# The eighth product of each group of eight on 128 rows in place of 64

## The chip, the cores and the metric

One core of a Trainium2 chip runs the kernel. The metric is the device time of one execution in microseconds (us), and lower is better. Several executions of the kernel before are given by their median; one further execution was recorded by the hardware profiler, and all rows below come from that one.

## What is computed

A recurrence over 768 steps (4 batches, 8 heads, head size 40) gives a matrix x of 3072 tokens by 320 features. Two dense layers follow.

```python
def _moe_ref(x, w_in, w_out):           # layer 1: 320 -> 2048 -> 320
    h = x @ w_in
    g = np.where(h >= 1.0, h, np.where(h <= -1.0, 0.0, (h + 1.0) ** 2 / 4.0))
    return g @ w_out

def _moe2_ref(x, w1, w2, w3, w_out):    # layer 2: 320 -> 3 x 768 -> 320
    h = np.maximum(np.maximum(x @ w1, x @ w2), x @ w3)
    return h @ w_out
```

All data is float32, and the result is float32.

## The kernel before

The recurrence is worked in 24 chunks of 32 steps (`front` and `back`, called from `build` for each chunk). Its products are small: many of them use a part of the TensorE array only, with 32, 40, 64, 96 or 104 rows and 32 or 40 columns (lines 462, 587, 607, 629, 664 and 684). A long run of small VectorE operations for each chunk (lines 487 to 513) belongs to it too.

The dense layers are done in a split form. A float32 operand is written as a high part and a low part in TensorE's rounded float32 type, and a product is the sum of high by high, high by low and low by high. For the 320 input features this makes a group of eight products that add up in one PSUM tile. Features 0 to 127 and 128 to 255 take two full slices of 128 rows each. The last 64 features stand in slice 4 of the weights, with the high part on rows 0 to 63 and the low part on rows 64 to 127; the activations hold the same 64 features twice, on rows 0 to 63 and again on rows 64 to 127 (the last 64 columns are copied behind the others before the transpose, at the end of `back` for layer 1 and by a second small DMA in `moe2`). So one product over 128 rows, the third in the list, gives both high by high and low by high for the last 64 features. The eighth product adds high weights by low activations for them, on rows 0 to 63 only.

Layer 1 (`moe1`) takes 256 tokens at a time, in 12 units. Each unit has 16 groups of eight (line 818, moving operand of 256 columns), in eight pairs; a pair is followed by an activation on ScalarE (line 824), a square (line 825 or GpSimd), a VectorE operation (line 826), the split of the result into gH and gL, and 12 products of line 840 that add into two output tiles. That is 192 groups in all. Layer 2 (`moe2`) takes 512 tokens at a time, in 6 units. Each has 18 groups of eight (line 954, 512 columns, 108 groups in all), three for each of six column blocks; ScalarE and VectorE form the maximum of the three and its high and low part (fH, fL, held in the memory of the layer-1 weights, so that the profile calls them "wi"), and line 980 multiplies them with the output weights, 18 products for each of 4 token blocks.

The order of the work is fixed when the program is built. A planner (`Plan`) gives each task a duration and starts tasks in a list order on every engine; a group of eight is entered with 8 x 109 ns in layer 1 (line 821) and 8 x 216 ns in layer 2 (line 956). The order that comes out is written into each engine's stream, and engines wait for one another by semaphores. In idle stretches of the plan the kernel issues filler products on the identity matrix (line 1009), without waits. Groups of layer 1 stand between the recurrence's products in TensorE's stream; the last unit of layer 1 and then layer 2 follow when the recurrence is done.

Of the kernel before, what the change touches and what calls it, by code (L numbers as in the profile page):

```python
# [210 lines left out]
def act(n):  # L211
    return 94 + n * 0.833
# [6 lines left out]
def dve(n):  # L219
    return 68 + n / 0.96  # L220
# [6 lines left out]
def pool(n):  # L227
    return 98 + n * 2.2


def ev(n):

    return (("ACT", acp(n)), ("DVE", dve(n)))
# [6 lines left out]
class Kernel:  # L240
# [557 lines left out]
    def moe1(self, u):  # L798
        nc, P = self.nc, self.P
        i2 = u % 2  # L800
        xk = [("xH", i2, c) for c in range(2)] + [("xL", i2, c) for c in range(2)]
        wi, wo = self.wi, self.wo
        og = [Group("out") for _ in range(2)]
        self.hm = []
        for mp in range(8):
            g = Group("b6" if u == 11 else "h")
            j = (u * 8 + mp) % 2
            for mm in range(2):
                m = mp * 2 + mm

                def hm(e, m=m, mm=mm, g=g):
                    p = self.bank[g.bank][:, mm * 256:(mm + 1) * 256]
                    ms = slice(m * 128, (m + 1) * 128)
                    xH, xL = self.xH[i2], self.xL[i2]
                    seq = [(wi[:, 0, ms], xH[:, 0]), (wi[:, 1, ms], xH[:, 1]), (wi[:, 4, ms], xH[:, 2]), (wi[:, 2, ms], xH[:, 0]),
                           (wi[:, 3, ms], xH[:, 1]), (wi[:, 0, ms], xL[:, 0]), (wi[:, 1, ms], xL[:, 1]), (wi[0:64, 4, ms], xL[0:64, 2])]
                    for i, (a, b) in enumerate(seq):
                        nc.tensor.matmul(p, a, b, start=(i == 0), stop=(i == 7))  # L818

                f = m // 4  # L820
                self.hm.append(P.add((("PE", 8 * 109.0),), hm, r=xk + [("wi", kt, f) for kt in range(5)], g=[g]))
            q = self.q[j]
            bv = lambda g=g: self.bank[g.bank].rearrange("p (a b) -> p a b", a=2)
            P.add((("ACT", act(512)),), lambda e, q=q, bv=bv: nc.scalar.activation(q, bv(), AF.Relu, bias=self.half, scale=0.5), w=[("q", j)], g=[g])  # L824
            P.add((("ACT", act(512)), ("POOL", pool(512))), lambda e, q=q: nc.scalar.square(q, q) if e == "ACT" else self.tt(e, q, q, q, ALU.mult), w=[("q", j)])  # L825
            P.add((("DVE", dve(512)),), lambda e, q=q, bv=bv: nc.vector.scalar_tensor_tensor(q, bv(), 1.0, q, ALU.max, ALU.min), w=[("q", j)], g=[g])  # L826
            P.add((("ACT", act(512)),), lambda e, q=q, j=j: self.copy(e, self.gH[j], q), r=[("q", j)], w=[("gH", j)])
            P.add((("POOL", pool(512)), ("DVE", dve(512)))[u == 11:], lambda e, q=q, j=j: self.tt(e, self.gL[j], q, self.gH[j].bitcast(F32), ALU.subtract),
                  r=[("q", j), ("gH", j)], w=[("gL", j)])
            for mm in range(2):  # L830
                m = mp * 2 + mm

                def om(e, m=m, mm=mm, j=j):
                    gH, gL = self.gH[j], self.gL[j]
                    for tg in range(2):
                        p = self.bank[og[tg].bank][:, 0:DM]
                        ts = slice(tg * 128, (tg + 1) * 128)
                        seq = [(gH[:, mm, ts], wo[:, m, 0]), (gH[:, mm, ts], wo[:, m, 1]), (gL[:, mm, ts], wo[:, m, 0])]
                        for i, (a, b) in enumerate(seq):
                            nc.tensor.matmul(p, a, b, start=(m == 0 and i == 0), stop=(m == 15 and i == 2))  # L840

                P.add((("PE", 6 * 136.0),), om, r=[("gH", j), ("gL", j), ("wo", m, 0), ("wo", m, 1)], w=["moe1"], g=og)
        for tg in range(2):
            c = u * 2 + tg
            xt = self.x2n[0]
            P.add(ev(320), lambda e, tg=tg, xt=xt: self.copy(e, xt, self.bank[og[tg].bank][:, 0:DM]), w=["x2n"], g=[og[tg]], bonus=1e6)
            self.dma(self.x2d[c], xt, r=["x2n"], w=[("x2d", c)], bonus=1e6)
# [66 lines left out]
    def moe2(self, u):  # L914
# [27 lines left out]
        for m in range(6):  # L942
            ms = slice(m * 128, (m + 1) * 128)
            k2 = (u * 6 + m) % 2
            early = u == 0 and m == 0
            gs = [Group("a" if early else "b6") for _ in range(3)]
            for j in range(3):
                def mm(e, j=j, ms=ms, g=gs[j]):
                    p = self.bank[g.bank]
                    w, yH, yL = tl["w3"], tl["yH"][i2], tl["yL"][i2]  # L950
                    seq = [(w[:, j, 0, ms], yH[:, 0]), (w[:, j, 1, ms], yH[:, 1]), (w[:, j, 4, ms], yH[:, 2]), (w[:, j, 2, ms], yH[:, 0]),
                           (w[:, j, 3, ms], yH[:, 1]), (w[:, j, 0, ms], yL[:, 0]), (w[:, j, 1, ms], yL[:, 1]), (w[0:64, j, 4, ms], yL[0:64, 2])]
                    for i, (a, b) in enumerate(seq):
                        nc.tensor.matmul(p, a, b, start=(i == 0), stop=(i == 7))  # L954

                t = P.add((("PE", 8 * 216.0),), mm, r=yk + [("w3", j, kt, m // 3) for kt in range(5)] + ([] if early else ["moe1"]), g=[gs[j]])
                if self.mm:
                    t.deps.add(self.mm)
                self.mm = t
            P.add((("ACT", act(512)),), lambda e, k2=k2, gs=gs: self.copy(e, tl["s1"][k2], self.bank[gs[0].bank]), w=[("s1", k2)], g=[gs[0]])  # L960
            P.add((("DVE", dve(512)),), lambda e, k2=k2, gs=gs: self.tt(e, tl["s2"][k2], tl["s1"][k2], self.bank[gs[1].bank], ALU.max), r=[("s1", k2)], w=[("q", k2)], g=[gs[1]])
            P.add((("DVE", dve(512)),), lambda e, k2=k2, gs=gs: self.tt(e, tl["s1"][k2], tl["s2"][k2], self.bank[gs[2].bank], ALU.max), r=[("q", k2)], w=[("s1", k2)], g=[gs[2]])
            sm = sl[m]
            t = P.add((("ACT", act(512)),), lambda e, k2=k2, m=sm: self.copy(e, tl["fH"][:, m], tl["s1"][k2]), r=[("s1", k2)], w=[("fH", sm)])
            if u < 2:
                t.deps.update(self.hm)
            P.add((("DVE", dve(512)),), lambda e, k2=k2, m=sm: self.tt(e, tl["fL"][:, m], tl["s1"][k2], tl["fH"][:, m].bitcast(F32), ALU.subtract),
                  r=[("s1", k2), ("fH", sm)], w=[("fL", sm)])
# [240 lines left out]
```

## Time and profile before

| | |
|---|---|
| median of 3 executions | 1240.98 us (1238.32 to 1241.63) |
| the profiled execution | 1236.07 us |
| its span, first to last instruction | 1234.3 us |
| TensorE matmul busy | 1108.8 us, 90% |
| TensorE weight loads busy | 924.8 us, 75% |
| VectorE busy | 817.2 us, 66% |
| ScalarE busy | 719.7 us, 58% |
| GpSimd busy | 385.5 us, 31% |

In the profile PE is the matmul side of TensorE, PEld its weight load side, DVE is VectorE, ACT ScalarE, POOL GpSimd, SPq the queue that issues DMAs. L818 is line 818 of the kernel. "128*128" before a shape gives the rows and columns of the array that an instruction uses. PE's matmuls are pipelined: each row shows a start and a duration, and the durations overlap, so the spacing of starts tells the rate. PEclk is the granted clock of TensorE as a share of its full 2.4 GHz; 0.50 is the level of 1.2 GHz.

### The profile page before, as it was taken

To read this page: it belongs to the slowest core of one execution; us is meant where nothing else is said; L and a number is where in the kernel's file an instruction comes from. 1 tells how busy PE (TensorE), PEld (TensorE's weight loads), DVE (VectorE), ACT (ScalarE), POOL (GpSimd) and SP (SyncE) were. 2 spreads that over 40 slices of the span, in tenths; PEclk is the share of its full clock that TensorE was granted. 3 is DMA by queue.
4 is the path that set the end of the run, shared out by engine and by line. 5 is a ranking of instruction groups with operands and counts; after the bars stand their busy time and mean duration, and the time that the engine had idled before them with its cause. 6 is when DMAs were issued, how large, how long until landed. Compare 5 with 4: busy or idle time off the path is not lost.

```text
span 1234.3 us, 36564 instructions
## 1 busy us (share of the span) xinstructions
PE 1108.8 (90%) x15477; PEld 924.8 (75%) x15477; DVE 817.2 (66%) x1613; ACT 719.7 (58%) x1557; POOL 385.5 (31%) x425
## 2 busy tenths in 40 slices
PE   7577789888888969998989989999999999999996
PEld 7477677777777858787878878888886776767765
DVE  6799979897999869985989869873242322222221
ACT  5557787678787767876778677877561221212111
POOL 5574424432243713454323723333151000000000
PEclk9798899899999988998989999999999999999998
DMA  9654312222332242323432132210250100100000
GB/s 235 169 135 110 98 45 66 66 77 46 86 103 70 58 119 57 97 66 89 120 84 57 47 82 61 66 31 16 69 167 12 47 26 22 42 6 22 1 22 24
DMA packets 66973, 86.96 MB, mean 70 GB/s; under 512 B 37233, under 2 KB 52721, under 8 KB 66801
## 3 DMA queue, kind: packets, MB, share of 16 engines
q1 hardware_dynamic: 66656, 84.48, 25.7%
q8 instruction: 123, 2.02, 0.7%
q14 instruction: 50, 0.40, 0.1%
q10 hardware_dynamic: 144, 0.07, 0.0%
HBM read 56.40 MB, written 16.32 MB: 59 GB/s over the span
## 4 chain that ended last, share of the span: by engine, by line
PE 43%; DVE 28%; issue 8%; DMA 8%; ACT 7%; POOL 4%; SPq 2%; DVEq 0%; POOLq 0%; ACTq 0%
PE bank L954 19%; PE bank L818 7%; PE bank L980 5%; PE bank L840 5%; DVE itmp L505 4%; DVE KBZ L424 3%; DVE ir L508 3%; DVE itmp L509 2%; DVE q L826 2%; SPq L272 2%; DMA JW<-wd 2%; ACT VUZ L255 1%; DMA rn<-in_r 1%; PE bank L438 1%; DVE T L512 1%
## 5 line engine op out<-in xcount | busy, mean ns | idle before, releaser
L840 PE MATMUL bank<-wo,gH 128*128 128x320 f32 x768 | 188.0, 331 | 0.3 <-ACT x2n L255 0.3
L818 PE MATMUL bank<-xH,wi 128*128 128x256 f32 x960 | 162.1, 299 | 0.0
L269 POOL TENSOR_TENSOR gL<-q,gH 128x512 fp32r<-128x512 f32 x87 | 116.6, 1344 | 133.4 <-ACT gH L255 96.6
L818 PE MATMUL bank<-xL,wi 128*128 128x256 f32 (+1 forms) x576 | 137.5, 316 | 0.0
L818 PEld LDWEIGHTS bank<-xH,wi 128*128 128x128 f32 x960 | 128.5, 191 | 10.6 <-issue 0.2
L840 PEld LDWEIGHTS bank<-wo,gH 128*128 128x128 f32 x768 | 125.6, 192 | 10.6 <-issue 0.7
L954 PE MATMUL bank<-wi,w 128*128 128x512 f32 (+1 forms) x432 | 121.5, 419 | 0.0
L840 PE MATMUL bank<-wo,gL 128*128 128x320 f32 x384 | 119.2, 310 | 0.0
L818 PEld LDWEIGHTS bank<-xL,wi 128*128 128x128 f32 (+1 forms) x576 | 95.1, 189 | 26.1 <-issue 0.9
L505 DVE TENSOR_TENSOR itmp<-T,lp 128x256 f32<-128x256 f32 (+6 forms) x216 | 105.4, 488 | 5.5
L954 PEld LDWEIGHTS bank<-wi,w 128*128 128x128 f32 (+1 forms) x432 | 76.9, 187 | 42.6 <-issue 27.5
L438 PE MATMUL bank<-ident,KBZ 128*104 128x128 f32 x384 | 59.2, 311 | 48.8 <-DVE KBZ L424 30.7
L269 DVE TENSOR_TENSOR q<-s,bank 128x512 f32<-128x512 f32 x36 | 24.8, 688 | 114.3 <-PE bank L954 114.3
L255 ACT CAST wi<-s 128x512 fp32r<-128x512 f32 x36 | 22.5, 625 | 133.4 <-DVE s L269 133.4
L826 DVE SCALAR_TENSOR_TENSOR q<-bank,q 128x512 f32<-128x512 f32 x96 | 65.2, 681 | 44.5 <-ACT q L825 27.9
L824 ACT ACTIVATE q<-bank,half 128x512 f32<-128x512 f32 x96 | 65.6, 688 | 45.1 <-PE bank L818 44.3
L438 PEld LDWEIGHTS bank<-ident,KBZ 128*104 128x104 f32 x384 | 49.4, 148 | 54.9 <-DVE KBZ L424 20.5
L508 DVE TENSOR_REDUCE ir<-itmp 128x16 f32<-128x256 f32 (+6 forms) x216 | 79.6, 369 | 5.2
L1009 PE MATMUL bank<-ident 128*128 128x128 bf16 x1221 | 79.9, 227 | 1.4 <-ACT un L255 1.2
L269 DVE TENSOR_TENSOR s<-q,bank 128x512 f32<-128x512 f32 x36 | 24.7, 687 | 81.5 <-PE bank L954 81.5
L1009 PEld LDWEIGHTS <-ident 128*128 128x128 bf16 x1221 | 76.1, 103 | 3.1 <-issue 1.9
L424 DVE STREAM_TRANSPOSE KBZ<-t 128x1280 f32<-128x1280 f32 x24 | 65.2, 2715 | 19.1 <-DMA t<-pk 9.9
(171 smaller groups left out, 2348.0 us busy)
## 6 DMA issues: line engine op xcount, KB each, us to landing
JW<-in_moe_w SPq DMA_DIRECT2D x12, 384.0 KB
raw<-in_moe_w_out SPq DMA_DIRECT2D x14, 320.0 KB
JW<-in_w SPq DMA_DIRECT2D x24, 160.0 KB
t<-in_v SPq DMA_DIRECT2D x48, 80.0 KB
pk<-in_k SPq DMA_DIRECT2D x24, 160.0 KB
pb<-in_b SPq DMA_DIRECT2D x24, 160.0 KB
pa<-in_a SPq DMA_DIRECT2D x24, 160.0 KB
rn<-in_r SPq DMA_DIRECT2D x96, 40.0 KB
```

The costliest lines, as they stand in the source:

```text
L269: (self.nc.vector if eng == "DVE" else self.nc.gpsimd).tensor_tensor(*a)
L424: P.add((("DVE", 1460.0),), lambda e: nc.vector.transpose(self.lanes(kb), t1.rearrange("p t e -> p e t")), r=t1k, w=[("KB", i2)] + self.kz ...
L438: nc.tensor.transpose(p[0:104, j * 128:(j + 1) * 128], kb[:, q * 4 + j, :], self.ident)
L505: op(n, lambda e, tv=tv, k0=J + 1 + k0, k1=J + 1 + k1, shape=shape, c0=c0, c1=c0 + 4 + ns: mul(tv, T[:, k0:k1, c0 + 4:c1].unsqueeze(2).to_ ...
L508: op(n, lambda e, tv=tv, rv=rv[:, k0:k1]: nc.vector.tensor_reduce(rv, tv, axis=AX.X, op=ALU.add), ["itmp"], ["ir"])
L818: nc.tensor.matmul(p, a, b, start=(i == 0), stop=(i == 7))
L824: P.add((("ACT", act(512)),), lambda e, q=q, bv=bv: nc.scalar.activation(q, bv(), AF.Relu, bias=self.half, scale=0.5), w=[("q", j)], g=[g])
L826: P.add((("DVE", dve(512)),), lambda e, q=q, bv=bv: nc.vector.scalar_tensor_tensor(q, bv(), 1.0, q, ALU.max, ALU.min), w=[("q", j)], g=[g])
L840: nc.tensor.matmul(p, a, b, start=(m == 0 and i == 0), stop=(m == 15 and i == 2))
L954: nc.tensor.matmul(p, a, b, start=(i == 0), stop=(i == 7))
L980: nc.tensor.matmul(p, a, b, start=(m == n == 0), stop=(m == 5 and n == 2))
L1009: nc.tensor.matmul(self.bank[idle[1]][:, 0:128], w[:, 0:128], w[:, 0:128], start=True, stop=True)
```

## The change

In both layers the eighth product of the group reads rows 0 to 127 of both operands in place of rows 0 to 63. The added rows multiply the low part of the weights with the low part of the activations; both are in memory already, since the third product reads the same weight rows and the low activations are written on all 128 rows. Nothing else differs, the planner's figures included.

```diff
-   (wi[:, 3, ms], xH[:, 1]), (wi[:, 0, ms], xL[:, 0]), (wi[:, 1, ms], xL[:, 1]), (wi[0:64, 4, ms], xL[0:64, 2])]
+   (wi[:, 3, ms], xH[:, 1]), (wi[:, 0, ms], xL[:, 0]), (wi[:, 1, ms], xL[:, 1]), (wi[:, 4, ms], xL[:, 2])]
...
-   (w[:, j, 3, ms], yH[:, 1]), (w[:, j, 0, ms], yL[:, 0]), (w[:, j, 1, ms], yL[:, 1]), (w[0:64, j, 4, ms], yL[0:64, 2])]
+   (w[:, j, 3, ms], yH[:, 1]), (w[:, j, 0, ms], yL[:, 0]), (w[:, j, 1, ms], yL[:, 1]), (w[:, j, 4, ms], yL[:, 2])]
```

## Rows read from the trace of the kernel before

**Rows 1.** The page's busy time by engine, and its strip of TensorE's clock.
```profile
PE 1108.8 (90%) x15477; PEld 924.8 (75%) x15477; DVE 817.2 (66%) x1613; ACT 719.7 (58%) x1557; POOL 385.5 (31%) x425
...
PEclk9798899899999988998989999999999999999998
```

**Rows 2.** Busy time by stage: window, its length, then each engine, clock, DMA.
```profile
152.00:845.00 693.00, 621.73 (x11192) 541.61 (x11190) 582.14 (x1207) 515.14 (x1142) 268.63 (x298) 0.96 0.27 71
845.00:907.00 62.00, 62.00 (x712) 54.72 (x711) 18.04 (x30) 38.56 (x83) 19.18 (x19) 1.00 0.25 71
...
907.00:1224.00 317.00, 316.64 (x1392) 228.10 (x1392) 86.41 (x132) 70.64 (x137) 14.56 (x15) 1.00 0.10 29
1224.00:1235.00 11.00, 0.00 (x0) 0.00 (x0) 0.00 (x0) 0.10 (x1) 0.00 (x0) 0.62 0.19 64
```

**Rows 3.** The chain that ended last, shares by line: 845 to 1234, then 152 to 845.
```profile
by line: PE bank L954 60.9%; PE bank L980 17.1%; PE bank L818 7.5%; PE bank L840 7.4%; PE bank L929 1.5%; PE bank L930 0.7%; PE bank L544 0.6%; PE bank L684 0.4%; PE bank L664 0.2%; PE bank L1009 0.2%; PE bank L587 0.2%; PE bank L607 0.2%; 
...
by line: issue 11.9%; PE bank L818 8.3%; DVE itmp L505 5.5%; PE bank L840 5.1%; DVE KBZ L424 5.1%; DVE ir L508 3.8%; DVE itmp L509 3.6%; DVE q L826 3.5%; SPq L272 2.8%; DMA rn<-in_r 2.3%; PE bank L438 2.2%; ACT VUZ L255 2.0%; ACT KBZ L255 1
```

**Rows 4.** PE in order of time, layer 2: start, us, line, operation, tiles, shapes.
```profile
1120.04 1.15 PE L980 MATMUL bank<-wo,wi 128*128 128x320 f32 x6
1121.03 1.32 PE L954 MATMUL bank<-yH,w 128*128 128x512 f32 x5
1122.19 1.04 PE L954 MATMUL bank<-yL,w 128*128 128x512 f32 x3
1123.16 5.55 PE L980 MATMUL bank<-wo,wi 128*128 128x320 f32 x36
...
1130.67 1.40 PE L954 MATMUL bank<-yH,w 128*128 128x512 f32 x5
1131.91 1.04 PE L954 MATMUL bank<-yL,w 128*128 128x512 f32 x3
```

**Rows 5.** Weight loads by form, 907 to 1234: busy, mean ns, idle time before.
```profile
L954 PEld LDWEIGHTS bank<-yL,w 128*128 128x128 f32 x108 | 20.3, 188 | 4.3
L954 PEld LDWEIGHTS bank<-wi,w 64*128 64x128 f32 x54 | 9.9, 183 | 19.8 <-issue 19.8
L954 PEld LDWEIGHTS bank<-yL,w 64*128 64x128 f32 x54 | 9.9, 183 | 19.1 <-issue 19.1
```

**Rows 6.** PE in order of time, three stretches of the last units of layer 1.
```profile
873.14 0.85 PE L818 MATMUL bank<-xH,wi 128*128 128x256 f32 x5
873.84 0.71 PE L818 MATMUL bank<-xL,wi 128*128 128x256 f32 x3
874.47 0.84 PE L818 MATMUL bank<-xH,wi 128*128 128x256 f32 x5
...
875.78 0.56 PE L840 MATMUL bank<-wo,gH 128*128 128x320 f32 x2
...
876.33 0.45 PE L840 MATMUL bank<-wo,gH 128*128 128x320 f32 x2
...
876.76 0.75 PE L818 MATMUL bank<-xH,wi 128*128 128x256 f32 x5
877.36 0.71 PE L818 MATMUL bank<-xL,wi 128*128 128x256 f32 x3
```

**Rows 7.** PE in order of time, from a full product to small ones.
```profile
846.10 0.31 PE L840 MATMUL bank<-wo,gL 128*128 128x320 f32 x1
846.34 0.81 PE L587 MATMUL bank<-VUZ,AL 104*32 104x40 f32 x64
```

**Rows 8.** Waits, 152 to 845: VectorE's longest, PE's longest (total us, times, longest).
```profile
DVE ln L269 <- PE bank L462: 18.5, 14, 5.1
...
PE bank L438 <- DVE KBZ L424: 18.3, 11, 4.8
```

**Rows 9.** Windows before and in a stretch of half clock, columns as in rows 2.
```profile
216.30:226.50 10.20, 7.50 (x220) 6.44 (x220) 9.99 (x22) 5.83 (x15) 6.60 (x8) 1.00 0.29 85
226.50:236.80 10.30, 8.99 (x98) 8.41 (x99) 9.68 (x18) 6.23 (x14) 3.57 (x6) 0.50 0.17 39
```

## The prediction

> **What bounds the kernel now.** I read the page first: TensorE's matmul side is busy for 90% of the span and no other engine comes near [rows 1]. That is an average, so the busy time by stage comes next [rows 2]. It shows three stages that matter. From 907 to 1224 us, layer 2, PE is busy 316.6 of 317 us while VectorE has 86 and ScalarE 71. From 845 to 907, the end of layer 1, PE is busy without a gap and VectorE is at 18 of 62. From 152 to 845 the recurrence and layer 1 run together: PE 621.7 of 693 us (90%) and VectorE 582.1 (84%), two engines that are loaded almost alike. After 1224 only the last copy and the output's transfers are left, which the change doesn't touch. The chain of waits says the same: from 845 on its shares are PE lines almost alone (L954 60.9%, L980 17.1%), but from 152 to 845 L818 has 8.3% of it beside many VectorE lines and 11.9% "issue", time whose cause the profile doesn't name [rows 3].
>
> A busy PE is not a PE at its peak, so the third view is PE in order of time, where spacing of starts is the rate. The change adds no instruction, wait or transfer and moves none: it alters 192 products of L818 and 108 of L954 in place. Operands are ready at the same point, because the third product of the group reads the same weight rows.
>
> **The change, part by part: layer 2.** Take the group that starts at 1121.03, right after a full product of L980 [rows 4]. Its first five products take 1122.19 - 1121.03 = 1.16 us, 0.232 each: that is the spacing of full 128-row products. The last three take 1123.16 - 1122.19 = 0.97 us until the next instruction starts, where three full ones would take 0.70. So the 64-row product loses 0.28 us: some of it before it starts, some until its successor starts. The weight load side shows where: before each of the 108 loads with 64 rows it sat idle, 19.8 + 19.1 us in total, 0.36 us per load, against 4.3 us before 108 loads of 128 rows of the same tile, 0.04 each [rows 5]. A second loss follows: a group whose predecessor ended in a 64-row product takes 1131.91 - 1130.67 = 1.24 us for its first five spacings, 0.08 more than the 1.16 above [rows 4]. The first spacing alone, along the whole timeline, puts this second loss at 0.10 us, as in layer 1 below, and it occurs behind 104 of the 108 groups (85 followed by L954, 16 by L980, 3 by L840); the other four are followed by transposes.
>
> If the eighth product behaves like the seventh, the group takes 8 x 0.232 = 1.86 us. The saving is 108 x 0.28 + 104 x 0.10 = 30.2 + 10.4 = 40.6 us. All of it lies on PE in a stage where PE never waits, so it should come off the end one to one. What could eat it: per column block VectorE has three operations and ScalarE two, and by the stage's sums they fill 86 and 71 of 317 us [rows 2]; with 276 us left they are still under a third. I keep 36 to 42 us.
>
> **End of layer 1, 845 to 907.** In the groups from 873.14 on [rows 6], the last three products take 874.47 - 873.84 = 0.63 us. The full spacing is read from the group behind L840: 877.36 - 876.76 = 0.60 for five, 0.12 each (0.118 with more digits on the timeline). Three would be 0.35, so the loss is 0.28 us again. The second loss is 0.70 - 0.60 = 0.10 us (873.14 to 873.84 against 876.76 to 877.36), and the same in the first pair of L840 behind a group, 0.56 against 0.45 us. Here 24 groups: 18 are followed by L818 or L840 (0.38), 4 by full transposes (0.28), 2 by small products (0.19, below): 6.8 + 1.1 + 0.4 = 8.3 us, on a PE that never idles. I keep 6 to 9.
>
> **Recurrence with layer 1, 152 to 845.** 168 groups lie here. Counted along the timeline, 94 are followed by L818 or L840, 29 by transposes on full rows, and 45 by the recurrence's small products. For the last kind part of the loss stays: from a full product of L840 to the small ones of L587 the start is 0.24 us off [rows 7], where a full successor comes after 0.15, so 0.09 of the 0.28 is the price of those small products themselves, and 0.19 is saved. Sum: 94 x 0.38 + 29 x 0.28 + 45 x 0.19 = 35.7 + 8.1 + 8.6 = 52.4 us of PE time. How much of that reaches the end? Above: all, 52. Below: the chain puts 8.3% of 693 = 57.5 us on L818, some 43 groups at 1.33 us [rows 3, 6], and 43 x 0.31 = 13 us (0.31 is 52.4 / 168); a path that shifts to VectorE could halve that, 5. In between stands VectorE's load: today the busiest engine gets 90% of the stretch [rows 2]; VectorE at the same 90% would need 582 / 0.90 = 647 us, a gain of 46. Both ends wait on each other (VectorE for PE's small products, PE for VectorE's transposes [rows 8]), so shorter PE steps also bring VectorE's work forward, but not all of it. I take the middle of 13 and 46 less 1 or 2 us for the clock (fourth rival), 28 us; 5 to 52 for the range.
>
> **The sum.** 40.6 + 8.3 + 28 = 77 us. Against the profiled execution that is 1236.07 - 77 = 1159 us. That execution lies 4.9 us under the median of the runs shown, and under the lowest of them, so I add 1 and say 1160.
>
> **A rule against it.** The loads of 64 and of 128 rows take 183 and 188 ns [rows 5], so by the load alone there is nothing to win. The Trainium skill, "TensorE: Matmul & The Clock Gate", section "LDWEIGHTS (loading the stationary operand)", says that a weight load's time goes by its columns and that one of 32 rows takes as long as one of 128; taken alone it gives no change, which is the third rival. The trace agrees on the duration, and shows the idle time beside it that the rule doesn't speak of.
>
> **The rivals.** First, VectorE holds the middle stage: PE gains 52 us there and waits them away in front of the recurrence's transposes, the wait that is PE's longest now [rows 8]. Then 5 us come from the middle and the sum is 40.6 + 8.3 + 5 = 54, 1182 us. For it: VectorE's 84%, and its part in the chain. Against: its own longest wait is for PE (18.5 us).
>
> Second, PE holds the middle stage alone: all 101 us of PE time come off, 1236 - 101 = 1135 us. For it: PE's 90%, and the "issue" in the chain may hide waits for PE. Against: VectorE would then be at 582 / 641 = 91%.
>
> Third, the change doesn't do what it says: the idle time before the 64-row load belongs to the last product of a group (its end is awaited by ScalarE, its successor writes another bank), not to the 64 rows. Then nothing moves, 1236 to 1241 us. Against: L840 and L980 change banks every three products without such a gap, and the loss begins before the eighth product starts, while the end of a group could only show behind it.
>
> Fourth, on the other side: slower through the clock. PE finishes earlier in the middle stage and idles more, and its clock is then granted at 0.5 more often. In the trace a stretch of 10.2 us in which PE was busy 7.5 is followed by 10.3 us at 0.50, the level of 1.2 GHz, with the same products at half the rate [rows 9]. In the middle the mean is 0.96 [rows 2], so some 55 us ran at half clock (2 x 0.04 x 693) and cost about 27. With 52 us less to do PE's share would be (622 - 52) / (693 - 28) = 86%, not far from today. To undo 77 us and come out 0.3% slower would take over 160 us more at half clock, a mean of about 0.84 there; that is the point from which this rival decides. In layer 2 PE has no gap and the clock can't fall for this reason.
>
> **How the numbers follow.** Forecast 62 in 100 (1145 to 1172 us); VectorE holds 18 (1172 to 1190); PE alone 15 (1134 to 1145); no effect 3; slower 2. The predicted time is the forecast's, 1160. The range takes in the first two rivals and the bounds of the three stages: lowest 1236 - (42 + 9 + 52) = 1133, highest 1236 - (36 + 6 + 5) = 1189. I give 1136 to 1190. 0.3% of this time, 3.7 us, is about what a measurement can tell from no change: faster 0.95, within it 0.03, slower 0.02.
>
> **What would show it.** Right: no 64-row form among L818's and L954's products; spacing 0.23 in layer 2 and 0.12 in layer 1 through the whole group, so 1.86 and 0.95 us per group; no idle time before the loads; layer 2's stage shorter by about 40 us with PE still full. In the middle stage VectorE's share up to about 87% and fewer waits for PE. Wrong: an eighth product that still starts late (third rival), a middle stage as long as before with more PE idle at the transposes of L438 (first), or PEclk well under 0.96 there (fourth). If the layer 2 stage shrank by much less than 36 us with ScalarE or VectorE waits ahead of PE, the cover that I counted on there is gone.

## The result and the profile after

| | before | after |
|---|---|---|
| median of 4 executions | 1240.85 us | 1186.86 us (1183.3 to 1188.7) |
| ratio, 95% interval | | 0.9565 (0.9538 to 0.9591) |
| the profiled execution, its span | 1236.07, 1234.3 | 1187.38, 1185.6 |

The change takes 54 us off (4.4%). The forecast was 1160, in a range of 1136 to 1190: the time lies inside, near the upper end, and the gain is two thirds of the 81 us that the forecast puts between it and the median. It is not in the band of the forecast itself (1145 to 1172) but in that of the first rival, VectorE holds (1172 to 1190). Where the time came off is seen in the busy time by stage (window, its length, each engine's busy us, then TensorE's clock, share of the DMA engines, GB/s). The borders answer to those of [rows 2]: the recurrence's last chunk begins 2.5 us later than before, and layer 2's first product stands at 902.8 in place of 909.0.

```profile
152.00:847.50 695.50, 584.05 (x11202) 534.82 (x11201) 585.24 (x1209) 516.46 (x1145) 271.46 (x299) 0.95 0.27 71
847.50:901.00 53.50, 53.21 (x707) 51.47 (x706) 17.14 (x30) 37.65 (x81) 18.12 (x18) 1.00 0.28 78
901.00:1175.00 274.00, 274.00 (x1391) 236.83 (x1389) 88.29 (x132) 70.26 (x136) 15.22 (x16) 1.00 0.12 35
1175.00:1186.00 11.00, 0.12 (x1) 0.00 (x0) 0.00 (x0) 0.57 (x2) 0.00 (x0) 0.72 0.20 64
```

Measured from instruction to instruction: from layer 2's first product to the last product of all it is 272.0 us where it was 314.3, 42.3 less. From the recurrence's last VectorE transpose (line 424) to layer 2's first product it is 93.7 where it was 102.4, 8.7 less. Up to that transpose it is 809.1 where it was 806.6, 2.5 more. So 42.3 + 8.7 - 2.5 = 48.5 us, all but 0.2 of the 48.7 between the two spans. The transposes, before and after (shortest, median and longest in ns, then first and last start in us):

```profile
L424 DVE STREAM_TRANSPOSE KBZ<-t x24: 2677/2714/2761, 42.2 to 806.6; 128x1280 f32<-128x1280 f32 x24
...
L424 DVE STREAM_TRANSPOSE KBZ<-t x24: 2671/2699/2790, 42.7 to 809.1; 128x1280 f32<-128x1280 f32 x24
```

In these two profiles the stage from 152 us on, in which the forecast put 28 us, gave nothing.

The products themselves do what the forecast says. PE in order of time, layer 2 and then the end of layer 1 (start, us, line, tiles, shapes):

```profile
1083.16 1.31 PE L954 MATMUL bank<-yH,w 128*128 128x512 f32 x5
1084.31 0.85 PE L954 MATMUL bank<-yL,w 128*128 128x512 f32 x3
1084.99 1.04 PE L980 MATMUL bank<-wo,wi 128*128 128x320 f32 x6
...
872.68 0.75 PE L818 MATMUL bank<-xH,wi 128*128 128x256 f32 x5
873.27 0.51 PE L818 MATMUL bank<-xL,wi 128*128 128x256 f32 x3
873.62 0.75 PE L818 MATMUL bank<-xH,wi 128*128 128x256 f32 x5
```

Layer 2: five products take 1084.31 - 1083.16 = 1.15 us and three take 0.68, against 0.97 in [rows 4], so a group takes 1.83 us. Layer 1: 0.59 and 0.35, against 0.70 and 0.63 in [rows 6], a group 0.94. The idle time before the weight loads is gone too: the loads by form in layer 2 (busy, mean ns, idle before) have no 64-row form any more, and before these loads the weight side sits idle for 0.04 us each in every form, where [rows 5] has 0.36 before those with 64 rows.

```profile
L954 PEld LDWEIGHTS bank<-wi,w 128*128 128x128 f32 x432 | 80.7, 188 | 18.7
L954 PEld LDWEIGHTS bank<-yH,w 128*128 128x128 f32 x270 | 50.0, 188 | 9.7
L954 PEld LDWEIGHTS bank<-yL,w 128*128 128x128 f32 x162 | 30.4, 188 | 6.4
```

Where the recurrence's stage lost its gain stands in its waits (us in total, times, longest) and in the chain that ended last there, both from 152 to 845 us:

```profile
PE bank L438 <- DVE KBZ L424: 28.4, 11, 6.4
...
DVE ln L269 <- PE bank L462: 16.9, 12, 5.1
...
by line: issue 10.9%; DVE itmp L505 6.8%; DVE KBZ L424 6.2%; DVE ir L508 4.8%; DVE itmp L509 4.4%; DVE q L826 4.2%; PE bank L818 3.9%; ACT VUZ L255 3.3%; SPq L272 3.3%; PE bank L438 2.9%; DVE lp L474 2.8%; PE bank L840 2.7%; DVE T L512 2.2%
```

PE waits 28.4 us for VectorE's transpose, where it waited 18.3 [rows 8]; VectorE's own longest wait hardly changed, 16.9 for 18.5. In the chain L818 went from 8.3% to 3.9%, and VectorE's lines grew (L505 from 5.5 to 6.8, L424 from 5.1 to 6.2) [rows 3]. In the window 152 to 845 PE's busy time fell from 621.7 to 581.6 us and VectorE's stayed, 582.1 and 584.8: the way through VectorE takes as long as before. Its waits say why. Summed over all lines of the waits view in this window they are 83.1 us before and 83.0 after: for TensorE 27.3 and 22.7, for ScalarE 26.7 and 28.5, for transfers 18.7 and 20.4, for GpSimd 10.2 and 11.2. So before the change VectorE stood waiting for TensorE itself for 27 us only, and the 5 us that went from these waits came back in the others.

### The profile page after: what moved, and what is told of

The parts are those of the page before. It is cut to its first block, busy times and chain, and to the rows that moved or that the text cites. A ratio compares the mean times of both kernels' runs of the same rounds, so it can differ in the third digit from the quotient of the medians.

```text
span 1185.6 us, 36564 instructions
## 1 busy us (share of the span) xinstructions
PE 1020.4 (86%) x15477; PEld 924.4 (78%) x15477; DVE 822.5 (69%) x1613; ACT 720.0 (61%) x1557; POOL 388.0 (33%) x425
## 4 chain that ended last, share of the span: by engine, by line
PE 35%; DVE 34%; ACT 10%; issue 8%; DMA 6%; POOL 3%; SPq 2%; DVEq 0%; ACTq 0%; POOLq 0%
PE bank L954 17%; PE bank L980 5%; DVE itmp L505 5%; PE bank L818 4%; DVE KBZ L424 4%; PE bank L840 4%; DVE ir L508 3%; DVE itmp L509 3%; DVE q L826 2%; ACT VUZ L255 2%; SPq L272 2%; DVE lp L474 2%; PE bank L438 2%; DVE T L512 2%; ACT q L824 1%
## 5 line engine op out<-in xcount | busy, mean ns | idle before, releaser
L840 PE MATMUL bank<-wo,gH 128*128 128x320 f32 x768 | 183.5, 325 | 1.9 <-ACT x2n L255 1.9
L269 POOL TENSOR_TENSOR gL<-q,gH 128x512 fp32r<-128x512 f32 x87 | 117.4, 1354 | 134.5 <-ACT gH L255 106.4
L818 PE MATMUL bank<-xH,wi 128*128 128x256 f32 x960 | 158.0, 295 | 0.1
L818 PEld LDWEIGHTS bank<-xH,wi 128*128 128x128 f32 x960 | 130.7, 194 | 3.2 <-DVE q L826 0.4
L840 PEld LDWEIGHTS bank<-wo,gH 128*128 128x128 f32 x768 | 126.8, 193 | 5.8 <-ACT x2n L255 2.9
L840 PE MATMUL bank<-wo,gL 128*128 128x320 f32 x384 | 119.8, 312 | 0.0
L438 PE MATMUL bank<-ident,KBZ 128*104 128x128 f32 x384 | 63.4, 328 | 60.6 <-DVE KBZ L424 39.7
L505 DVE TENSOR_TENSOR itmp<-T,lp 128x256 f32<-128x256 f32 (+6 forms) x216 | 104.4, 484 | 5.5
L438 PEld LDWEIGHTS bank<-ident,KBZ 128*104 128x104 f32 x384 | 53.3, 157 | 66.5 <-DVE KBZ L424 29.8
L954 PE MATMUL bank<-wi,w 128*128 128x512 f32 x432 | 102.7, 396 | 0.0
L818 PE MATMUL bank<-xL,wi 128*128 128x256 f32 x576 | 101.7, 286 | 0.8 <-DVE xL L269 0.8
L954 PEld LDWEIGHTS bank<-wi,w 128*128 128x128 f32 x432 | 80.7, 188 | 18.7
L818 PEld LDWEIGHTS bank<-xL,wi 128*128 128x128 f32 x576 | 84.0, 194 | 1.0 <-DVE xL L269 1.0
L508 DVE TENSOR_REDUCE ir<-itmp 128x16 f32<-128x256 f32 (+6 forms) x216 | 79.7, 369 | 5.2
L255 ACT CAST gH<-q 128x512 fp32r<-128x512 f32 x96 | 58.9, 617 | 34.4 <-DVE q L826 20.2
L424 DVE STREAM_TRANSPOSE KBZ<-t 128x1280 f32<-128x1280 f32 x24 | 65.0, 2709 | 20.8 <-DMA rn<-in_r 15.2
```

The source lines that it names most:

```text
L255: self.nc.scalar.copy(out, in_)
L269: (self.nc.vector if eng == "DVE" else self.nc.gpsimd).tensor_tensor(*a)
L424: P.add((("DVE", 1460.0),), lambda e: nc.vector.transpose(self.lanes(kb), t1.rearrange("p t e -> p e t")), r=t1k, w=[("KB", i2)] + self.kz ...
L438: nc.tensor.transpose(p[0:104, j * 128:(j + 1) * 128], kb[:, q * 4 + j, :], self.ident)
L505: op(n, lambda e, tv=tv, k0=J + 1 + k0, k1=J + 1 + k1, shape=shape, c0=c0, c1=c0 + 4 + ns: mul(tv, T[:, k0:k1, c0 + 4:c1].unsqueeze(2).to_ ...
L508: op(n, lambda e, tv=tv, rv=rv[:, k0:k1]: nc.vector.tensor_reduce(rv, tv, axis=AX.X, op=ALU.add), ["itmp"], ["ir"])
```

## The experiments

The theory to be tested has two parts. First, the loss sits in the step between a 64-row and a 128-row product, on both sides. Second, the recurrence's stage is held by VectorE's stream with its waits, so that TensorE time saved there turns into idle time. Rivals: for the first, the end of a group or each 64-row product by itself; for the second, TensorE's clock, which ran at half for 65 us of that stage where it was 51 before, or a bound that the engines share. Every ratio is against runs of the kernel before on the same chip in the same series.

| kernel | median us | ratio (95% interval) |
|---|---|---|
| layer 2 only | 1195.18 | 0.9655 (0.9612 to 0.9697) |
| layer 1 only | 1223.88 | 0.9888 (0.9846 to 0.9930) |
| changed, half groups in layer 1 | 1179.73 | 0.9527 (0.9489 to 0.9564) |
| changed, less VectorE work | 1151.46 | 0.9283 (0.9244 to 0.9322) |
| before, less VectorE work | 1212.23 | 0.9788 (0.9754 to 0.9822) |
| before, 64-row product fourth | 1245.37 | 1.0052 (1.0031 to 1.0073) |
| 96 rows | 1184.92 | 0.9573 (0.9537 to 0.9609) |
| changed, with fillers | 1181.94 | 0.9561 (0.9520 to 0.9602) |
| changed, more VectorE work | 1255.85 | 1.0149 (1.0128 to 1.0169) |
| before, more VectorE work | 1308.82 | 1.0591 (1.0549 to 1.0633) |
| 64-row products side by side | 1208.89 | 0.9770 (0.9734 to 0.9805) |
| changed, planned anew | 1197.58 | 0.9680 (0.9657 to 0.9703) |

**One layer at a time.** Each of the two kernels has one of the two changed lines.

> The change in layer 2 alone. In the changed kernel layer 2's stage is 42 us shorter and the stage from 152 to 845 us is not shorter at all. If stages add up, this alone gives 40 to 43 us less than before, some 1199 us, and leaves the middle stage as it was. If the two layers' gains lean on each other, it is less than 38.

> The change in layer 1 alone, 192 groups. Theory (VectorE's stream with its waits sets the recurrence's stage): only the 24 groups behind it count, 6 to 9 us less than before, 1232 to 1235 us, with 168 groups' 52 us turned into idle time of TensorE. Rival (TensorE shares the bound): 25 us or more, 1216 or less.

Layer 2 alone gives 45 us by the medians, 43 by the ratio, with the recurrence's stage as before (its last transpose at 808.1 us, 806.6 before). Layer 1 alone gives 16 us by the medians, 14 by the ratio with some 5 to either side. That is more than the 6 to 9 of the theory and less than the 25 of its rival. From the recurrence's end to layer 2 it took 93.8 us, 8.6 less than before, so the rest, 4 us in its profile, would come from the recurrence. Four profiles of kernels with layer 1 changed and the recurrence as it was put the last transpose at 802.4 (layer 1 only), 803.3 (side by side), 805.2 (96 rows) and 809.1 us (the change), mean 805.0; without it stand 806.6 and 808.1. The stage's gain is about 2 us, with a scatter larger than that.

**Where the loss sits.** First the 64-row product stands fourth in the group, not last:

```diff
+   seq = seq[0:3] + seq[7:8] + seq[3:7]
```

> The kernel before with the 64-row product fourth in each group of eight in both layers, not eighth; the last is a product on 128 rows. Theory (the loss belongs to the step between 64 and 128 rows, on both sides of the product): the same losses inside the group, 1236 to 1244 us, no different from before. Rival (the loss belongs to the end of a group, its write-out or the next bank): a group ends on a full product and the loss is gone or still at its end; if gone, some 1187.

Here are the loads by form in layer 2, as above:

```profile
L956 PEld LDWEIGHTS bank<-yL,w 64*128 64x128 f32 x54 | 9.9, 183 | 19.2 <-issue 19.2
L956 PEld LDWEIGHTS bank<-wi,w 64*128 64x128 f32 x54 | 9.9, 183 | 19.7 <-issue 19.7
```

The 38.9 us of idle time are where they were in [rows 5], and the time from layer 2's first product to the last is 314.4 us, 314.3 before. So the end of a group has no part in it. The total is 7 us over before, a little above what was expected, and all of it is in the recurrence's stage (last transpose at 814.7). A reason that fits is that a group which ends on a full product now pays a second step into the recurrence's small products, 0.09 us as in [rows 7], 45 times; in this run's trace the last full product starts 0.21 us ahead of such small ones and 0.12 ahead of a full one. But 45 times 0.09 us is 4 of the 7 us, it was not tried by itself, and if TensorE's time in this stage only turned into idle time, as the theory has it, it should not come out at all. So this excess stays open. VectorE's waits in the window 152 to 845 are 87.8 us here, 83.1 before, most of the difference for ScalarE (31.4, 26.7).

Then the 64-row products of two groups are put side by side in layer 2, with layer 1 changed:

```diff
+   if (u * 18 + m * 3 + j) % 2:
+       seq = seq[7:8] + seq[0:7]
```

> Layer 1 changed; in layer 2 the 64-row product stays, but in every second group of eight it comes first, so that it stands right behind the 64-row product that ends the group ahead. Theory (the loss is the step between 64 and 128 rows, not the 64-row product): a pair of groups pays once, 0.38 us less per pair, about 45 pairs that touch, 17 us less than with layer 1 changed alone (1224), 1205 to 1209. Rival (each 64-row product pays by itself): 1222 to 1226.

```profile
L956 PEld LDWEIGHTS bank<-yL,w 64*128 64x128 f32 x54 | 8.4, 184 | 10.9 <-issue 10.9
L956 PEld LDWEIGHTS bank<-wi,w 64*128 64x128 f32 x54 | 8.3, 184 | 10.9 <-issue 10.9
```

There are as many 64-row products as before, but the idle time before their loads is 21.8 us in place of 38.9, and the kernel is 15 us faster than the one with layer 1 changed alone. The step is what costs, not the product.

Last, the count of rows: 96 in place of 128 (half of the added terms is left out).

```diff
-   (wi[:, 4, ms], xL[:, 2])]
+   (wi[0:96, 4, ms], xL[0:96, 2])]
...
-   (w[:, j, 4, ms], yL[:, 2])]
+   (w[0:96, j, 4, ms], yL[0:96, 2])]
```

> The eighth product on rows 0 to 95 in both layers, so that a half of the added terms is left out. The recurrence's products on 96 and 104 rows follow full ones in the trace without a gap where they use all columns (transposes on 104 rows). Theory: what counts is the half of the array's rows, and 96 rows are taken like 128: 1183 to 1191 us, as the changed kernel. Rival: any count under 128 costs the same as 64: 1237 to 1244.

```profile
L954 PEld LDWEIGHTS bank<-wi,w 96*128 96x128 f32 x54 | 10.1, 188 | 2.5
L954 PEld LDWEIGHTS bank<-yL,w 96*128 96x128 f32 x54 | 10.1, 188 | 2.1
```

4.6 us of idle time before 108 loads, 0.04 us each, as for full loads; the time is that of the change. A product on 96 rows follows and precedes one on 128 without the loss. "TensorEngine Tiling (Array Packing)" of the Trainium skill says in "Tiling Modes", key properties, that a change of the tiling mode drains TensorE; its list of modes has one of 64 rows. The traces agree, in that the loss comes with each step between the forms `128*128` and `64*128`; they show its price here, 0.28 us for the way in and out and 0.10 for the product behind it, and not the drain itself.

**What holds the recurrence's stage.** First VectorE's work is cut, by taking four terms of each inner sum of the inverse:

```diff
+   tv, shape, ns = tv[:, :, :, 0:4], [128, k1 - k0, 4, 4], 4
```

> The changed kernel with the inner sums of the recurrence's triangular inverse cut to four terms each (lines 505 and 508, 216 instructions each, same count and order, the result is not the inverse): about 100 us of VectorE busy time, some 80 in the recurrence's stage. Theory (VectorE holds that stage): it shrinks until TensorE is at about 90% of it, 582 / 0.90 = 647 in place of 695 us, so 40 to 55 us off, with some more ahead of it: 1130 to 1150 us. Rival (the clock at half, or transfers, took the gain): it stays within 10 us of the changed kernel, above 1175.

> The kernel before with the same cut of the inverse's inner sums on VectorE (result not the inverse). With the change the cut took 35 us (1187 to 1151), 30 of it in the recurrence's stage. Theory (VectorE and TensorE share that stage; the full VectorE hides what the change gives there): without the change TensorE is at 622 us there and lets little of the cut through, 5 to 20 us, so 1220 to 1235, and the change is worth 70 to 85 us here in place of 54. Rival (VectorE alone): the cut takes 35 us here too, 1205, and the change is worth 54 again.

The cut is smaller than was expected: 64 us of VectorE time by the page (822.5 to 758.7), not 87 to 100. The changed kernel gains 35 us from it, the kernel before 26. The changed kernel ends just over the theory's 1150. So VectorE's work lies on the way through the stage in both, and the rival of this run, that the clock or the transfers alone took the gain (above 1175), is out. But 64 us of work bring 35, so other ways are close behind. In the changed kernel, to a point as far behind the last transpose as 845 us is without the cut (811), VectorE is busy 60 us less and waits 23 us more (106.4 for 83.0): 12 more for ScalarE, 7 each for TensorE and GpSimd, 2 less for transfers. The change is worth 61 us by the medians of this pair (63 by the ratios; the two ran in different series) and 54 in the other; that lies between theory and rival, and with an interval of some 6 us to either side it shows no more than a weak pull of TensorE. Here is the window from 152 to 800 us, before with the cut, then changed with the cut:

```profile
152.00:800.00 648.00, 592.31 (x10859) 517.11 (x10858) 509.93 (x1164) 496.42 (x1100) 257.29 (x291) 0.97 0.29 76
...
152.00:800.00 648.00, 561.82 (x10981) 515.52 (x10980) 519.08 (x1190) 503.03 (x1112) 260.52 (x294) 0.96 0.29 76
```

PE at 91% and VectorE at 79% in the first, and still the change takes only 8 us off this stage (last transpose 783.2 to 775.2). A busy share doesn't name the bound.

Then VectorE's work is raised: each reduction of line 508 is done twice.

```diff
-   nc.vector.tensor_reduce(rv, tv, axis=AX.X, op=ALU.add)
+   [nc.vector.tensor_reduce(rv, tv, axis=AX.X, op=ALU.add) for _ in range(2)]
```

> The changed kernel with each of the 216 inner reductions of the inverse (line 508, 0.369 us) done twice on VectorE, the second for nothing: 80 us more VectorE time, some 65 of it in the recurrence's stage. Taking 87 us away took 35 us off. Theory (VectorE's stream with its waits is the longest way through that stage, other ways are close behind): added time comes out nearly whole, 60 to 80 us, 1247 to 1267. Rival (several engines share the stage evenly): as with the cut, some 30 to 40, 1217 to 1227.

> The kernel before with the same doubled reductions. Theory: VectorE's way is longer still, TensorE's idle time takes up everything that the change gives in the recurrence's stage, so the change is worth layer 2 and the end of layer 1 alone, 48 to 52 us against the doubled kernel with the change. Rival (the two engines share): the change is worth as much as without the doubling, 54, or more.

The page has 80.8 us more for line 508 (79.7 to 160.5), and 65 more for VectorE as a whole (822.5 to 887.4), since some other lines took less. The changed kernel takes 69 us more, the kernel before 72. Nearly all that is added to VectorE comes out at the end, in both: its stream is the longest way through the stage.

```profile
152.00:845.00 693.00, 557.88 (x10441) 513.61 (x10434) 598.23 (x1294) 476.60 (x1052) 249.74 (x280) 0.90 0.27 70
```

The clock moved with it: the changed kernel now spends 133 us of this window at half clock, not 65. That this made the stage longer is not seen in VectorE's stream: to 906 us, as much further on as the last transpose (870.0 for 809.1), it is busy 66 us more and waits 10 us less, and its waits for TensorE are 23.8 us for 22.7. The theory holds against its rival, the even share. In this pair the change is worth 53 us, between what theory and rival expected, so this second question is left open by it.

Next the opposite end, TensorE's work in layer 1 halved in the changed kernel:

```diff
+   seq = seq[0:3] + seq[7:8]
...
-   nc.tensor.matmul(p, a, b, start=(i == 0), stop=(i == 7))
+   nc.tensor.matmul(p, a, b, start=(i == 0), stop=(i == 3))
```

> The changed kernel with four of the eight products of layer 1's groups left out (both low-part rows of the first 256 features and the low activations there), so the output lacks them: TensorE loses 192 x 4 x 0.118 = 91 us, 79 of it in the recurrence's stage. Theory: that stage stays within 5 us, the end of layer 1 gives up to 11 us, 1171 to 1181 in all. Rival (TensorE shares the bound there): about half of 79 and 11, 1136 us; TensorE alone: 1096.

```profile
152.00:845.00 693.00, 546.35 (x10671) 492.00 (x10671) 582.57 (x1209) 518.52 (x1150) 272.41 (x302) 0.89 0.27 72
```

7 us by the medians, 5 by the ratios, for 91 us of TensorE work. But the granted clock of the stage fell to 0.89, and PE's busy time to 546 from 582, 35 us and not 79: with fewer products the engine spent 154 us of the stage at 1.2 GHz. So this run shows that TensorE's saved work does not come out, and it cannot show alone whether that is VectorE or the clock.

For the clock there is the run with fillers ahead of the transposes of line 438:

```diff
+   w = self.ident.bitcast(BF16)
+   for j in range(32 if q == 0 else 0):
+       nc.tensor.matmul(p[:, 0:128], w[:, 0:128], w[:, 0:128], start=True, stop=True)
```

> The changed kernel with 32 filler products of 128 columns on the identity ahead of the recurrence's transposes of line 438, once in each of the 24 chunks, where TensorE most often waits for VectorE; nothing of the result changes. About 1.8 us of TensorE time per chunk. In the changed kernel 65 us of the recurrence's stage ran at half clock, 51 before. Rival (the clock took the gain back): with the clock up the stage is 10 us or more shorter, 1177 or less. Theory (VectorE's stream holds the stage): within 5 us, 1182 to 1192, whatever the clock does.

```profile
152.00:845.00 693.00, 613.42 (x12002) 565.89 (x12004) 584.41 (x1213) 519.18 (x1152) 273.07 (x302) 0.97 0.27 72
```

The clock came up from 0.95 to 0.97 (41 us at half, not 65). The ratio, 0.9561, is that of the change, 0.9565. The median lies 5 us lower, at the edge of what the theory gave, and the last transpose at 802.1, beside the earliest of the four named above (802.4). So 24 us less at half clock came with 5 us at the most. The fillers take TensorE time of their own, and 41 us stay at half, so the run does not give the clock's whole cost. But what the change added was 14 us at half clock, which is at most 7 us of TensorE work; that cannot have taken 28.

**A plan that spares VectorE.** The handicap of VectorE in the planner is raised, so that ScalarE gets some of the copies:

```diff
-BIAS = {"ACT": 400.0, "DVE": 1500.0, "POOL": 0.0, "PE": 0.0, "SP": 0.0}
+BIAS = {"ACT": 400.0, "DVE": 2500.0, "POOL": 0.0, "PE": 0.0, "SP": 0.0}
```

> The changed kernel with the planner's handicap for VectorE raised from 1500 to 2500 ns, so that some copies that may go to either engine go to ScalarE; the order of all engines is planned anew. By the planner's durations about 20 us leave VectorE and 21 come to ScalarE. Theory (VectorE holds the recurrence's stage): 5 to 15 us less than the changed kernel, 1172 to 1182. Rival (what the stage waits for is ScalarE's or GpSimd's turn as much, or the new order has other stalls): within 5 us or slower.

It is 11 us slower than the change (14 by the ratios), so the theory's 5 to 15 us of gain did not come. VectorE's busy time from 152 to 800 us is 534.9 us in place of 550.4, 15 less, and still the stage ends 7 us later (816.1 for 809.1), with the clock at 0.92. VectorE's waits from 152 to 845 us rose from 83.0 to 98.3: 17 us more for TensorE, 10 more for ScalarE, 9 less for transfers. What counts is VectorE's stream with its waits and its order, not its busy time alone. Which steps of the new order brought these waits was not followed.

## Why the prediction was right, and where not

The time lies in the range because the range was drawn around the first rival too. The forecast's own band, given 62 in 100, ends at 1172, and the time is in the band that was given 18. Two of the three terms came as forecast; the third did not.

**Layer 2**: 40.6 us forecast, 42.3 measured in the profile, 43 to 45 by the run with layer 2 alone. The two losses (0.28 and 0.10 us) were read from spacings of starts, and the stage had no other engine near; the cover that was named (VectorE and ScalarE under a third) held: 88 and 70 of 274 us.

**End of layer 1**: 8.3 forecast, 8.7 measured, with PE full through the stage.

**Recurrence with layer 1**: 28 forecast within 5 to 52, and 2 measured over six profiles, -2.5 in the profile of the change itself, under the lower bound (the run with layer 1 alone leaves some 5, with as much to either side). This is the term that was mis-sized, and it makes up nearly all the difference. The sign that was named for it, VectorE's share at about 87%, did not come: it stayed at 84%. The TensorE time did come off: PE was busy 40 us less in the stage (52 were worked out; 14 us more at half clock took back some 7). The step that failed is the conversion into time at the end. It took a share of the chain (43 groups at 0.31 us, 13 us) as what comes at least, halved it only for the lower bound, and went up from there by VectorE's busy share, as if an engine at 84% left 46 us of room. The runs showed what stands in its place. In the changed kernel 81 us more of reductions on VectorE bring 69, and 64 us less bring 35, so its stream is the longest way, and its 16% of idle time (111 us before) is made of short gaps and of 83 us of waits, for TensorE, ScalarE, transfers and GpSimd, whose sum the faster layer 1 did not move. Those for TensorE, 27 us before, are about all of the 28 that the forecast counted on, and 5 of them went. What stays open is why the other waits rose by as much, and the 7 us of the run with the 64-row product fourth. The first rival, "VectorE holds", named the right wait, PE at L438 for L424, and put the time at 1182, 54 us under the profiled execution; 54 us is what the medians show, and its 5 us for the middle fit the runs within their scatter.

**Rivals.** PE alone (1135) is out by the halved groups. That the loss belongs to a group's end is out by the fourth position (the prediction's own argument against it, banks changed every three products, is true of L840; L980 changes them after 15 or after 3). The clock moved as the fourth rival said, 51 to 65 us at half, but by a tenth of the 160 us that it would need. The rule that the prediction held against the change, on a weight load's columns, is true of the load: it went from 183 to 188 ns. The idle time beside it is what was worth 54 us.

**The sum against the median**: the profiled execution of before lay 4.8 us under its median and that of after at it, so the medians show 54 where the spans show 48.7. Forecasts from one execution carry that much.

## What to carry to other kernels

Read spacing of starts, not busy time, around each product whose row count falls to 64 among products on 128: here each such step cost 0.38 us, three times the 0.118 us spacing of a full product with 256 columns (way in, way out and the product behind). If the other rows hold data that do no harm (here they even add a term), take them; if not, put such products side by side, which in layer 2 gave back 15 of some 43 us. And before counting an engine's saved time in a stage shared with another, add up the other's waits for the first: here they were 27 us, and 5 of them went. Or add some work to the other: here that came out nearly whole, and the saving did not.

## What the runs showed of the hardware

A product on 96 rows costs no step beside those on 128 (0.04 us of idle time before its load), one on 64 rows does (0.36). With the 64-row product fourth, the starts in layer 1's groups are 0.21 us apart into it, 0.31 out of it, 0.22 behind the next product and 0.12 elsewhere. With half the products of layer 1 gone, TensorE's clock was granted at 0.89 in the stage in place of 0.95, and a saving of 79 us of products shortened its busy time by 35 only.
